# Four 64x64 tiles for strided attention and eight 64x32 tiles for two spans of local scores, with two PSUM banks in turn

## The chip, the cores and the metric

The kernel runs on one core of a Trainium2 chip. The metric is the device time of one execution in microseconds. Five engines work side by side: TensorE (PE in the rows; its weight loads are PEld), VectorE (DVE), ScalarE (ACT), GpSimd (POOL) and SyncE (SP), which here only issues DMAs. Each engine runs its own instructions in order; semaphores between them carry the dependencies.

## The reference: sparse attention, then a mixture of experts

Four batches of eight heads, 576 positions, head dimension 64. Heads 0 to 3 attend locally, to the last 32 positions; heads 4 to 7 attend with a stride, to earlier positions of the same remainder by 32. The 2304 rows that come out feed four experts.

```python
scores = scale * np.matmul(q, k.transpose(0, 1, 3, 2))
mask_local = (rel >= 0) & (rel < stride)
mask_strided = (rel >= 0) & (pos[None, :] % stride == pos[:, None] % stride)
scores = scores - np.max(scores, axis=-1, keepdims=True)
attn = np.exp(scores)
attn = attn / (np.sum(attn, axis=-1, keepdims=True) + 1e-09)
x = np.matmul(attn, v)                       # rearranged to (2304, 512)
h = np.maximum(x @ w1[e], 0.0)               # for each of 4 experts
out += p[:, e:e + 1] * (h @ w2[e])
```

## The kernel before

**Work.** Attention goes by 16 pairs of heads (4 batches x 4 pairs), in turn a local and a strided one. The two heads of a pair lie on partitions 0 to 63 and 64 to 127 of the tiles `qkL` and `qkS`, so a matmul of one head uses one half of TensorE's 128 rows. The experts are cut into 8 units of 512 hidden columns. The first 384 rows of x go through all 8 units while the attention of the other rows still runs (`plan_first`); the other 1920 rows follow in two parts after attention, with no attention in them.

**One pair.** `plan_pair` lays down, for each pair and for two parts of it (`gi`): the scores on TensorE into a PSUM bank of the pool `sc` (2 banks); on DVE the mask (which also empties the bank into `pm`) and the row maximum; the subtraction on DVE or POOL; the exponential on ACT; the row sum and its reciprocal on DVE; the normalization on DVE or POOL; a transpose (`tp`) on TensorE through the pool `ps` (2 banks), copied out by ACT or DVE; the values matmul (`pv`) into `ps`; and the copies out to `xh`, `xl` or `xr`.

**Tiles of the array.** In local scores a matmul has 64 rows and 32 columns; the two heads and two neighbouring blocks give four positions, (64h, 64h + 32i). In strided scores a matmul has 64x64 and head h stands at position (h, h): two positions. In strided values 54 of the 64 rows carry data; one part `gi` is one half `hf` of the rows, so its matmuls stand at (hf, 0) and (hf, 1): two positions. The part `gi` of strided scores (x in the changed code) and of strided values has one bank of its own.

**What sets the order.** Nothing is scheduled at run time. `Plan.walk` simulates the engines once while the kernel is built, with a cost for each operation, priorities in microseconds, banks in flight and a rule for taking turns between attention and experts on TensorE (`MIX`, `swing`, `ROW`), and writes out the instructions in the order of the simulated starts. The costs of the flexible operations also choose between DVE and POOL ("VP") and between ACT and DVE ("AD"). Early on it fills TensorE's waits with matmuls on zeros (`idle`, tile `wz`), up to `STEADY`.

**Names in rows.** A float32 matmul of attention is one row of the program but two instructions in the trace: 12 matmuls of the program are x24 in the trace. L494 is the local scores, L499 the strided scores, L556 the transposes, L583 the local values, L591 the strided values, L752 and L768 the experts' first and second matmuls over the first 384 rows, L921 those of the later parts, L1232 the zeros. Any matmul on the experts is called an expert matmul below.

Of the kernel before, what the change touches and what calls it, by code (L numbers as in the profile page):

```python
# [8 lines left out]
F32 = mybir.dt.float32  # L9
# [8 lines left out]
MIX = 0.8  # L18
# [5 lines left out]
LEAD = 11.15  # L24
LAG = 2.35
STEADY = 45.0
# [6 lines left out]
class Plan:  # L33
# [8 lines left out]
    DEEP = 1.3  # L42
    ROW = 1.51
# [3 lines left out]
    def __init__(self, banks, mix):  # L47
        self.ops = []
        self.writer = {}
        self.readers = {}  # L50
        self.banks = banks
        self.mix = mix
        self.swing = 2.0

    def add(self, eng, dur, fn, reads=(), writes=(), prio=0.0, bank=None, moe=False, cols=0, xfer=None, two=False, lead=None, lag=0.0):
# [7 lines left out]
        o.eng, o.dur, o.fn, o.prio, o.bank, o.moe = eng, dur, fn, prio, bank, moe  # L63
# [6 lines left out]
        o.idx = len(self.ops)  # L70
        pre = set()
# [33 lines left out]
    def walk(self):  # L105
# [31 lines left out]
        def fill(f, s, o):  # L137

            n = 0
            while True:  # L140
# [13 lines left out]
                if f + step > s and not forced:  # L154
# [9 lines left out]
        def when(o):  # L164
# [3 lines left out]
            if o.bank:  # L168
                n = len(allocs[o.bank[0]]) - self.banks[o.bank[0]]
                if n >= 0:  # L170
                    for p in self.readers.get(allocs[o.bank[0]][n], ()):
# [59 lines left out]
        while left:  # L231
# [20 lines left out]
            if e == "PE":  # L252
# [11 lines left out]
                if s < STEADY:  # L264
                    f = max(f, 1.07)
                    tag = next((t for t in allocs if not (o.bank and o.bank[0] == t) and clear(t, f) and not (began and t == "mo")), None)
# [6 lines left out]
            dur = took(o, e, s)  # L273
            if o.eng in self.FLEX:
# [26 lines left out]
            if o.bank:  # L301
                allocs[o.bank[0]].append(o.bank)
# [7 lines left out]
def attn_moe_kernel(  # L310
# [51 lines left out]
    const.tile([P, 8], F32, name="skew")  # L362
# [78 lines left out]
    def plan_pair(n):  # L441
# [11 lines left out]
        for gi in range(2):  # L453
            kb = (410, 213)[gi] if kd == "L" else 337
            add("SP", 0.65, lambda gi=gi: load_qk(n, gi), (), [f"qk{kd}{bf}{gi}"], zg[gi] - 16, xfer=((kb * 0.003, 128),), lead=lead)
# [5 lines left out]
        def pmv(g0, g1):  # L461
            if kd == "S":
                return pmx[:, g0:g1, 0:W]
            a = pmx[:, P * g0 + 1:P * g0 + 2]
            return bass.AP(a.tensor, a.offset, [list(a.ap[0]), [3 * P, (g1 - g0) // 3], [P + 32, 3], [1, W]])
# [12 lines left out]
        for gi, (g0, g1) in enumerate(GRP[kd]):  # L478
# [5 lines left out]
            def scores(key=key, gi=gi, g0=g0, g1=g1):  # L484
                s = bank(key)
                for g in range(g0, g1):
                    o = (g - g0) * W
                    for h in range(2):
                        a = slice(64 * h, 64 * h + 64)
                        if kd == "L":  # L490
                            o0, nq, _ = QKL[gi]
# [827 lines left out]
```

## Time and profile before

| | us |
|---|---|
| Median of 3 runs (804.46 to 805.23) | 804.83 |
| Profiled execution, its own time | 805.53 |
| Its span, first to last instruction | 803.7 |
| TensorE busy | 794.7 (99%) |
| VectorE busy | 612.9 (76%) |
| GpSimd busy | 357.3 (44%) |
| ScalarE busy | 330.4 (41%) |
| Share of TensorE in the chain that ended last | 96% |

TensorE is granted its full clock throughout (1.00 in every stretch asked for). A busy TensorE is not TensorE at its peak: small matmuls on few tiles of the array fill its time as well as large ones. So a gain is read from the time that passes between the first matmul of a piece and the first matmul of the next.

### The profile page before, as it was taken

What the parts mean: (1) busy time and instruction counts of PE and PEld (TensorE: products, weight loads), DVE (VectorE), ACT (ScalarE), POOL (GpSimd) and SP (SyncE); (2) the same over time, 40 slices, a digit from 0 to 9 for tenths busy, and PEclk for the clock granted to TensorE, in tenths of its full rate; (3) what the DMA queues carried; (4) which work ended last, traced back from release to release, by engine and by line L of the source; (5) the groups of instructions that cost most, each with busy time, mean ns of one, the idle gap of its engine ahead of it and who ended that gap; (6) DMA issues with size and microseconds to landing.
All of it is one profiled execution on the core that took longest, in us unless ns stands there. A gap on an engine that the chain in (4) does not pass through costs nothing.

```text
span 803.7 us, 13270 instructions
## 1 busy us (share of the span) xinstructions
PE 794.7 (99%) x5035; PEld 678.3 (84%) x5035; DVE 612.9 (76%) x871; ACT 330.4 (41%) x617; POOL 357.3 (44%) x277
## 2 busy tenths in 40 slices
PE   8999999999999999999999999999999999999998
PEld 5888888999889898888989888888888887888886
DVE  6888886875689776868687683868687878696986
ACT  3744646443336253444526361524131414232330
POOL 5442322932276451515244361526271808071762
PEclk9999999999999999999999999999999999999999
DMA  9675433348668696967764314838384747464625
GB/s 332 221 267 213 175 113 106 105 152 293 250 261 267 261 318 222 333 200 291 262 254 131 135 51 164 298 112 302 106 287 145 257 150 256 154 217 182 184 79 184
DMA packets 70400, 166.60 MB, mean 207 GB/s; under 512 B 5152, under 2 KB 23744, under 8 KB 70336
## 3 DMA queue, kind: packets, MB, share of 16 engines
q1 hardware_dynamic: 70192, 165.63, 58.8%
q8 instruction: 40, 0.66, 0.3%
q14 instruction: 24, 0.20, 0.1%
q10 hardware_dynamic: 144, 0.11, 0.0%
HBM read 105.94 MB, written 59.79 MB: 206 GB/s over the span
## 4 chain that ended last, share of the span: by engine, by line
PE 96%; DVE 2%; DMA 1%; ACT 1%; issue 0%; POOL 0%; DVEq 0%; ACTq 0%
PE mo L921 21%; PE mo L768 18%; PE ps L921 17%; PE sc L921 15%; PE mo L752 8%; PE sc L768 5%; PE ps L768 5%; PE ps L556 2%; PE ps L591 1%; PE sc L499 1%; DMA ring<-d23s 1%; PE sc L494 1%; PE ps L583 1%; PE mo L1232 1%; DVE wv L663 0%
## 5 line engine op out<-in xcount | busy, mean ns | idle before, releaser
L986 POOL TENSOR_TENSOR q<-q,q 128x512 f32<-128x512 f32 x41 | 60.9, 1494 | 143.2 <-DVE q L955 142.4
L768 PE MATMUL mo<-w2t,h 128*128 128x512 f32 x336 | 80.8, 389 | 0.0
L768 PEld LDWEIGHTS mo<-w2t,h 128*128 128x128 f32 x336 | 63.1, 188 | 13.0
L768 PE MATMUL mo<-w2t,hs 128*128 128x512 f32 x288 | 70.5, 396 | 0.0
L759 DVE SCALAR_TENSOR_TENSOR h<-c,h 128x448 fp32r<-128x448 f32 x48 | 61.3, 1305 | 2.4 <-ACT h L756 0.8
L768 PEld LDWEIGHTS mo<-w2t,hs 128*128 128x128 f32 x288 | 52.8, 188 | 11.0
L662 ACT ACTIVATE w2t<-raw 128x512 fp32r<-128x512 f32 x60 | 37.1, 630 | 41.9 <-PE mo L768 21.8
L663 POOL TENSOR_TENSOR a<-raw,a 128x512 fp32r<-128x512 f32 x19 | 29.8, 1570 | 52.8 <-DVE c L1124 48.0
L1035 DVE TENSOR_TENSOR acc<-sc,acc 128x512 f32<-128x512 f32 x58 | 39.2, 686 | 17.3 <-PE sc L921 17.2
L952 DVE TENSOR_TENSOR q<-ps,v 128x512 f32<-128x512 f32 x48 | 33.1, 690 | 24.9 <-PE ps L921 24.7
L777 DVE SCALAR_TENSOR_TENSOR acc<-mo,pr,acc 128x512 f32<-128x512 f32 x45 | 33.5, 745 | 22.3 <-PE mo L768 22.1
L943 ACT ACTIVATE v<-mo 128x512 f32<-128x512 f32 x48 | 28.6, 595 | 48.2 <-PE mo L921 48.2
L663 POOL TENSOR_TENSOR w2t<-raw,w2t 128x512 fp32r<-128x512 f32 x19 | 26.7, 1412 | 44.8 <-ACT w2t L662 44.8
L752 PE MATMUL mo<-xh,a 128*128 128x384 f32 x192 | 45.6, 341 | 0.0
L955 DVE SCALAR_TENSOR_TENSOR q<-q,pb 128x512 f32<-128x512 f32 x48 | 42.8, 892 | 1.6
L662 ACT ACTIVATE wv<-tmp 128x512 fp32r<-128x512 f32 x32 | 20.1, 632 | 54.6 <-POOL tmp L670 10.5
L768 PE MATMUL ps<-w2t,h 128*128 128x512 f32 x168 | 40.4, 389 | 0.0
L768 PE MATMUL sc<-w2t,h 128*128 128x512 f32 x168 | 40.4, 389 | 0.0
L981 ACT ACTIVATE Tb11h<-q 128x512 fp32r<-128x512 f32 x16 | 10.0, 628 | 71.5 <-DVE q L955 71.5
L663 DVE TENSOR_TENSOR w2t<-raw,w2t 128x512 fp32r<-128x512 f32 x41 | 35.1, 883 | 5.1 <-ACT w2t L662 5.1
L986 DVE TENSOR_TENSOR q<-q,q 128x512 f32<-128x512 f32 x23 | 32.7, 1421 | 6.7 <-POOL Tb21l L982 6.5
L768 PEld LDWEIGHTS sc<-w2t,h 128*128 128x128 f32 x168 | 31.5, 188 | 6.5
(270 smaller groups left out, 2109.0 us busy)
## 6 DMA issues: line engine op xcount, KB each, us to landing
raw<-in_w SPq DMA_DIRECT2D x30, 1024.0 KB, 6.1
qkS<-in_qk_strided SPq DMA_DIRECT2D x16, 329.0 KB, 6.5
out<-acc SPq DMA_DIRECT2D x18, 256.0 KB, 2.0
qkL<-in_qk_local SPq DMA_DIRECT2D x8, 400.0 KB, 6.5
vstL<-in_v_local SPq DMA_DIRECT2D x8, 384.0 KB, 7.0
vstS<-in_v_strided SPq DMA_DIRECT2D x8, 384.0 KB, 7.3
pb<-dp SPq DMA_DIRECT2D x5, 512.0 KB, 7.2
d17s<-s SPq DMA_DIRECT2D x4, 512.0 KB, 4.0
```

The costliest lines, as they stand in the source:

```text
L662: add("ACT", 0.62, lambda: nc.scalar.activation(out=hi(), in_=src(), func=AF.Copy), need, [name + "h"], z)
L663: add("VP", VP, lambda e: engine(e).tensor_tensor(out=lo(), in0=src(), in1=hi().bitcast(F32), op=ALU.subtract), need + [name + "h"], [name ...
L752: nc.tensor.matmul(pt[:, 0:TA], w[:, c % 2, (f % 2) * P:(f % 2) * P + P], (xl if i == 1 else xh)[c], start=j == 0, stop=j == 11)
L759: nc.vector.scalar_tensor_tensor(out=dst(), in0=src(), scalar=0.0, in1=hi().bitcast(F32), op0=ALU.max, op1=ALU.subtract)
L768: nc.tensor.matmul(pt, ht[f][:, ts], wt[f][:, cs], start=j == 0, stop=j == 11)
L777: nc.vector.scalar_tensor_tensor(out=a, in0=pt, scalar=sc, in1=a, op0=ALU.mult, op1=ALU.add)
L921: nc.tensor.matmul(pt, a[i == 2][:, j, f * P:f * P + P], skewed(b[i == 1][j], TH), start=bool(first) and n == 0, stop=True, skip_group_che ...
L943: add("ACT", TH2 / 1200 + 0.18, lambda: nc.scalar.activation(out=late["u"][i], in_=held[key][:, 0:TH2], func=AF.Copy), [key, "late3"], [f" ...
L952: add("DVE", DD, lambda: nc.vector.tensor_tensor(out=q(), in0=src(), in1=late["u"][i], op=ALU.add), [key, f"u{i}", "late3"], [tok], min(zz ...
L955: add("DVE", DD, lambda: nc.vector.scalar_tensor_tensor(out=q(), in0=q() if from_q else src(), scalar=0.0, in1=late["p"][:, c * TH2:c * TH ...
L986: add("VP", VP, lambda e: engine(e).tensor_tensor(out=dst[0](), in0=a[0](), in1=b[0](), op=ALU.subtract), [a[1], b[1]], [dst[1]], zz - 2.4)
L1035: add("DVE", DD, lambda i=i, key=key: nc.vector.tensor_tensor(out=acc[i], in0=held[key][:, 0:TH2], in1=acc[i], op=ALU.add), [key], tok, zd)
```

## The change

**Strided scores.** The two parts of a pair become one operation. It takes two `sc` banks at once, one for each head (that is, for each half of the rows). Each step issues four matmuls at four positions: part x at columns 64x, head h at rows 64h. The host lays out `qkS` accordingly: halves of the pair that were on x now come before the heads.

**Strided values.** The two parts become one operation too, with two `ps` banks, one for each half `hf` of the rows; each step issues matmuls at (hf, h), four positions.

**Local scores.** The first part of a pair covers two spans of three blocks (v = 0, 1); it takes two `sc` banks, one for each span, and the second span swaps the heads' column halves (`h ^ v`), so that eight 64x32 positions are used. The second part has one span and keeps four positions. The mask of the first part is now two instructions of 189 elements where one of 378 stood; transposes and values read the swapped halves.

**Sums.** The local row sum reads one more column, which holds 1e-9 from the start (two small memsets on POOL), and the separate addition of 1e-9 (16 instructions on DVE) is gone.

**The start.** The exponential's table is loaded by a dummy exponential after the masks' DMA is issued. The first block of w1 comes in two DMAs of half the size. In SP's order the first local pair's v and the first half of w1 now stand behind all four strided loads of q and k, before behind two of them. The second quarter of it that is split is now s3's, ahead of a12's.

**The plan.** `MIX`, `swing`, `ROW`, `STEADY`, `LEAD`, `LAG`, `DEEP` and the costs of attention's operations have other values; a switch from attention to experts costs 0.17 in the plan; at most ten zero matmuls are put in at a time beyond the start; and `SHIFT` moves the due times of 70-odd operations. The built program has 21 zero matmuls where it had 18. From the middle of the experts' first rows on (the last 3,050 of some 4,290 expanded rows) TensorE's program is the same.

```diff
-MIX = 0.8
+MIX = 0.85
+ZN = 30
+ZR0, ZR1 = 26.0, 24.0
-LEAD = 11.15
-LAG = 2.35
-STEADY = 45.0
+LEAD = 8.24
+LAG = 1.8
+STEADY = 30.04
+SHIFT = {
+    3: 5.5, 31: 1.9, 32: 1.8, 42: 1.7, 52: 10.9, 58: -4.8, 59: -4.8, 67: -4.8, 78: -7.5, 79: -14.4, 87: -6.6, 88: -3,
...
-    DEEP = 1.3
-    ROW = 1.51
+    DEEP = 1.27
+    ROW = 1.98
+    SWITCH = 0.17
+    FIRST = 10
+    SWING = 4.72
...
+            keys = [key]
+            if kd == "S":
+                keys = [("sc", n, "b", i) for i in range(2)] if gi == 0 else []
+            elif gi == 0:
+                keys = [("sc", n, "b", 0), ("sc", n, "b", 2)]
+
+            def scores(keys=keys, gi=gi, g0=g0, g1=g1):
+                ss = [bank(x) for x in keys]
+                if kd == "S":
+                    for o in range(0, 6 * W, W):
+                        for x in range(2):
+                            for h in range(2):
+                                a = slice(64 * h, 64 * h + 64)
+                                nc.tensor.matmul(
+                                    ss[h][64 * x:64 * x + 64, o:o + W], qkv[a, x, o:o + 64],
+                                    qkv[a, x, QKS + o:QKS + o + SR], start=True, stop=True)
+                    return
+                o0, nq, _ = QKL[gi]
+                for r in range(3):
+                    for v, s in enumerate(ss):
+                        for h in range(2):
                             for i in range(2):
-                                t = o0 + 96 * (2 * ((g - g0) // 3) + i) + 32 * (g % 3)
+                                a = slice(64 * h, 64 * h + 64)
+                                t = o0 + 96 * (2 * v + i) + 32 * r
+                                p = 64 * (h ^ v) + 32 * i
                                 nc.tensor.matmul(
-                                    s[64 * h + 32 * i:64 * h + 32 * i + 32, o:o + W], qkv[a, t:t + 32],
+                                    s[p:p + 32, r * W:r * W + W], qkv[a, t:t + 32],
                                     qkv[a, t + nq + 1:t + nq + 1 + W], start=True, stop=True)
-                        else:
-                            lhsT, rhs = qkv[a, gi, o:o + 64], qkv[a, gi, QKS + o:QKS + o + SR]
-                            nc.tensor.matmul(s[a, o:o + W], lhsT, rhs, start=True, stop=True)
...
-                    nc.vector.tensor_reduce(out=rows(sm, g0, g1), in_=pmv(g0, g1), op=ALU.add, axis=AX.X)
-                    nc.vector.tensor_scalar_add(out=r, in0=r, scalar1=1e-9)
+                    nc.vector.tensor_reduce(out=rows(sm, g0, g1), in_=pmv(g0, g1, 1), op=ALU.add, axis=AX.X)
...
+                if kd == "S":
+                    for j in range(6):
+                        for h in range(2):
+                            for hf in range(2):
+                                r, c0 = slice(64 * hf, 64 * hf + SR), 64 * (j % 2)
+                                nc.tensor.matmul(
+                                    oo[hf][64 * h:64 * h + 64, j * SR:j * SR + SR], vv[r, h, j, :],
+                                    pt[r, 3 * h + j // 2, c0:c0 + SR], start=True, stop=True)
+                    return
...
+        for j in range(2):
+            add("SP", 0.4, lambda j=j: load_w(which, u, slice(2 * j, 2 * j + 2)), (), [toks[j]], Z0 - (ZR0, ZR1)[j], xfer=((1.45, 256),), lag=LAG)
...
-        for src, nm in ((A11, "a11"), (A12, "a12"), (A21, "s3"), (A22, "a22")):
-            plan_quarter(src, "raw1", nm, z)
+        for src, nm, j in ((A11, "a11", 0), (A21, "s3", 0), (A12, "a12", 1), (A22, "a22", 1)):
+            plan_quarter(src, f"raw1{j}", nm, z)
...
         nc.scalar.dma_start(out=both, in_=c_masks)
+        nc.scalar.activation(out=warm[:, 0:1], in_=wz[:, 0:1], func=AF.Exp)
```

In the middle of attention, on TensorE before (`vstS` is the strided values' v, `qkL` and `qkS` local and strided q and k, `hs` the experts' hidden rows):

```order
209 L591 MATMUL ps<-pTS,vstS_241 64x54 x24
210 L768 MATMUL mo<-w2t,hs_223 128x512 x2
211 L768 MATMUL mo<-w2t,hs_227 128x512
212 L768 MATMUL mo<-w2t,hs_224 128x512 x2
213 L768 MATMUL mo<-w2t,hs_228 128x512
214 L556 MATMUL ps<-ident,pmL_242 128x128 x6
215 L494 MATMUL sc<-qkL_235 32x63 x12
216 L499 MATMUL sc<-qkS_237 64x54 x12
```

At about the same place now:

```order
218 L622 MATMUL ps<-pTS,vstS_241 64x54 x24
219 L529 MATMUL sc<-qkL_235 32x63 x12
220 L529 MATMUL sc<-qkL_234 32x63 x12
221 L630 MATMUL ps<-pTL,vstL_238 64x96 x8
222 L817 MATMUL mo<-w2t,hs_225 128x512 x2
223 L817 MATMUL mo<-w2t,hs_229 128x512
224 L817 MATMUL mo<-w2t,hs_226 128x512 x2
225 L817 MATMUL mo<-w2t,hs_230 128x512
226 L592 MATMUL ps<-ident,pmS_244 128x128 x3
227 L592 MATMUL ps<-ident,pmL_243 128x128 x3
228 L517 MATMUL sc<-qkS_237 64x54 x24
```

A pair's strided scores stand in one piece of 24 where they came as 12 and 12 in two places, and four pieces of attention follow one another before the experts' next turn.

On POOL before, from the first strided softmax to the low parts of the first w1 block (`a_77` is the quarter a11, `s_80` s3, `a_78` a12, `a_79` a22):

```order
18 L516 TENSOR_TENSOR pmS_244<-pmS_244,mx 128x6x54
19 L516 TENSOR_TENSOR pmL_243<-pmL_243,mx 128x2x3x63
20 L532 TENSOR_TENSOR pmS_244<-pmS_244,sm 128x6x54
21 L663 TENSOR_TENSOR a_77<-raw_202,a_77 128x512
22 L663 TENSOR_TENSOR a_78<-raw_202,a_78 128x512
23 L663 TENSOR_TENSOR s_80<-raw_202,s_80 128x512
24 L663 TENSOR_TENSOR a_79<-raw_202,a_79 128x512
```

The same place on POOL now:

```order
21 L562 TENSOR_TENSOR pmL_243<-pmL_243,sm 128x2x3x63
22 L547 TENSOR_TENSOR pmS_244<-pmS_244,mx 128x6x54
23 L562 TENSOR_TENSOR pmL_242<-pmL_242,sm 128x3x63
24 L562 TENSOR_TENSOR pmS_244<-pmS_244,sm 128x6x54
25 L547 TENSOR_TENSOR pmL_243<-pmL_243,mx 128x3x63
26 L707 TENSOR_TENSOR s_80<-raw_202,s_80 128x512
27 L707 TENSOR_TENSOR a_77<-raw_202,a_77 128x512
```

More softmax stands ahead of the first w1 quarter, s3's low part goes before a11's, and a22's has moved to DVE.

On ACT at the start, before:

```order
1 L1162 DMA both<-c_masks 128x432
2 L520 ACT_TABLE_LOAD
3 L520 ACTIVATE pmL_242<-pmL_242 128x2x3x63
4 L520 ACTIVATE pmL_242<-pmL_242 128x3x63
5 L433 ACTIVATE pTL<-ps 128x384 x2
```

and now:

```order
1 L1211 DMA both<-c_masks 128x432
2 L1212 ACT_TABLE_LOAD
3 L1212 ACTIVATE warm<-wz 128x1
4 L551 ACTIVATE pmL_242<-pmL_242 128x2x3x63
5 L551 ACTIVATE pmL_243<-pmL_243 128x2x3x63
6 L452 ACTIVATE pTL<-ps 128x384 x2
```

The table load stands in front of the dummy, whose operand is ready early, and no longer in front of the first exponential.

## Rows read from the trace of the kernel before

**Rows 1.** Stretches: length, busy us of PE, PEld, DVE, ACT, POOL (instructions), granted clock.

```profile
20.00:60.00 40.00, 39.23 (x591) 34.67 (x586) 35.46 (x84) 23.52 (x51) 20.02 (x22) 1.00 0.69 243
60.00:120.00 60.00, 60.00 (x945) 50.93 (x944) 51.58 (x116) 32.08 (x73) 17.92 (x24) 1.00 0.47 169
...
200.00:804.00 604.00, 598.90 (x2718) 509.51 (x2716) 459.08 (x571) 227.06 (x402) 271.90 (x185) 1.00 0.60 210
```

**Rows 2.** TensorE in order of time, 49 to 64: start, us, line, count.

```profile
49.85 0.53 PE L494 MATMUL sc<-qkL 64*32 64x63 f32 x24
50.32 0.91 PE L499 MATMUL sc<-qkS 64*64 64x54 f32 x24
51.16 0.96 PE L752 MATMUL mo<-xh,a 128*128 128x384 f32 x4
...
53.44 1.21 PE L583 MATMUL ps<-pTL,vstL 128*64 128x96 f32 x24
54.58 0.91 PE L499 MATMUL sc<-qkS 64*64 64x54 f32 x24
...
58.38 0.86 PE L494 MATMUL sc<-qkL 64*32 64x63 f32 x48
59.17 0.55 PE L556 MATMUL ps<-ident,pmL 128*128 128x128 f32 x3
...
61.77 1.43 PE L591 MATMUL ps<-pTS,vstS 54*64 54x54 f32 x48
63.12 1.19 PE L768 MATMUL mo<-w2t,hs 128*128 128x512 f32 x4
```

**Rows 3.** The same view, 117 to 128.

```profile
117.33 0.91 PE L591 MATMUL ps<-pTS,vstS 54*64 54x54 f32 x24
118.17 0.96 PE L752 MATMUL mo<-xh,a 128*128 128x384 f32 x4
...
127.30 0.55 PE L583 MATMUL ps<-pTL,vstL 128*64 128x96 f32 x8
127.78 0.55 PE L556 MATMUL ps<-ident,pmS 128*128 128x128 f32 x3
```

**Rows 4.** Stretches of L591 alone: length, busy us (matmuls under way), clock, DMA, GB/s.

```profile
19.30:19.82 0.52, 0.52 (x18) 1.00 1.01 380
19.82:20.00 0.18, 0.18 (x20) 1.00 1.04 389
```

**Rows 5.** L591 in 19 to 21: count, duration ns min/median/max, first and last start.

```profile
L591 PE MATMUL ps<-pTS,vstS x48: 218/218/258, 19.3 to 20.5; 54*64 54x54 f32 x48
```

**Rows 6.** DVE groups in the first 134 us: line, tiles, count, busy us, mean ns.

```profile
L510 DVE TENSOR_TENSOR pmS<-sc,both 128x324 f32<-128x324 f32 x16 | 7.7, 482 | 0.1
...
L510 DVE TENSOR_TENSOR pmL<-sc,both 128x378 f32<-128x378 f32 x8 | 4.3, 543 | 6.8 <-PE sc L494 6.8
...
L526 DVE TENSOR_SCALAR sm<-sm 128x3 f32<-128x3 f32 x8 | 3.2, 394 | 0.3
...
L510 DVE TENSOR_TENSOR pmL<-sc,both 128x189 f32<-128x189 f32 x8 | 2.8, 349 | 0.4 <-PE sc L494 0.3
L526 DVE TENSOR_SCALAR sm<-sm 128x6 f32<-128x6 f32 x8 | 1.9, 240 | 0.3
```

**Rows 7.** All engines in order of time, 8 to 20.

```profile
8.61 1.28 ACT L520 ACT_TABLE_LOAD   x1 [8.61 <-DVE pmL L516]
...
16.73 2.84 POOL L663 TENSOR_TENSOR a<-raw,a 128x512 fp32r<-128x512 f32 x2
...
18.07 0.42 PE L752 MATMUL mo<-xh,a 128*128 128x384 f32 x1
```

**Rows 8.** Waits of TensorE: line, releaser, us in total, times, longest.

```profile
PE ps L556 <- DVE xl L630: 0.3, 1, 0.3
PE ps L1183 <- DVE xl L630: 0.3, 1, 0.3
PE ps L556 <- POOL pmS L532: 0.2, 1, 0.2
```

More of the change, by code (lines that the diff above doesn't have):

```diff
@@ L70, in add @@
         o.idx = len(self.ops)
+        o.prio += SHIFT.get(o.idx, 0.0)
         pre = set()
@@ L153, in fill @@
                     need - o.cols) / 2400 / rate > rem - max(s - f, 0.0) - o.dur / rate
-                if f + step > s and not forced:
+                if f + step > s and not forced or not out and n >= self.FIRST:
                     return n, f
@@ L167, in when @@
                 t = max(t, wire - self.DEEP)
-            if o.bank:
-                n = len(allocs[o.bank[0]]) - self.banks[o.bank[0]]
+            for i, key in enumerate(o.bank):
+                n = len(allocs[key[0]]) - self.banks[key[0]] + i
                 if n >= 0:
-                    for p in self.readers.get(allocs[o.bank[0]][n], ()):
+                    for p in self.readers.get(allocs[key[0]][n], ()):
                         if p.start is None:
@@ L265, in walk @@
                     f = max(f, 1.07)
-                    tag = next((t for t in allocs if not (o.bank and o.bank[0] == t) and clear(t, f) and not (began and t == "mo")), None)
+                    tag = next((t for t in allocs if not (o.bank and o.bank[0][0] == t) and clear(t, f) and not (began and t == "mo")), None)
                     n, f2 = fill(f, s, o) if tag else (0, f)
@@ L273, in walk @@
             dur = took(o, e, s)
+            if e == "PE" and o.moe and last[e] is not None and not last[e].moe:
+                dur += self.SWITCH
             if o.eng in self.FLEX:
@@ L300, in walk @@
                     offer(x)
-            if o.bank:
-                allocs[o.bank[0]].append(o.bank)
+            for key in o.bank:
+                allocs[key[0]].append(key)
             out.append((s, o.idx, 0, fn))
@@ L537, in plan_pair @@
             vp = (dd, nel * 1.6e-3 + 0.22)
-            add("PE", 0.2 + ng * (0.107, 0.116)[c > 1], scores, [f"qk{kd}{bf}{gi}"], [key, tok], z + 3, key, cols=(4, 2)[c > 1] * nel)
-            add("DVE", dd, mask, [key, "mask" + kd], [tok], z + 3.2)
+            if kd == "S" and gi == 0:
+                add("PE", 0.9, scores, [f"qkS{bf}{i}" for i in range(2)], keys + [f"pmS{bf}{i}" for i in range(2)], z + 3, keys,
+                    cols=4 * nel)
+            elif kd == "L":
+                add("PE", (0.5, 0.46)[gi], scores, [f"qkL{bf}{gi}"], keys + [tok], z + 3, keys, cols=4 * nel)
+            for i, x in enumerate(keys if kd == "L" else [key]):
+                a0, a1 = (g0 + 3 * i, g0 + 3 * i + 3) if kd == "L" else (g0, g1)
+                add("DVE", (a1 - a0) * W / 960 + 0.15, lambda x=x, a0=a0, a1=a1: mask(x, a0, a1), [x, "mask" + kd], [tok], z + 3.2)
             add("DVE", dd, rmax, [tok], [tm], z + 3.4)
@@ L647, in attn_moe_kernel, with load_w @@
     NU = len(units)
-    def load_w(which, u):
+    def load_w(which, u, ks=slice(0, NKD)):
         e, f = units[u]
         src = w1[e, :, f * FH:(f + 1) * FH] if which == 1 else w2[e, f * FH:(f + 1) * FH, :]
-        nc.sync.dma_start(out=raws[which], in_=src.rearrange("(k p) f -> p k f", p=P))
+        nc.sync.dma_start(out=raws[which][:, ks], in_=src.rearrange("(k p) f -> p k f", p=P)[:, ks])
     def raw_quarter(i, j, which=1):
```

109 lines of the change are left out of this document (53 added, 56 removed), and 5 rows, old and new, of the table SHIFT.

## The prediction, made before the changed kernel was run

> **What bounds the kernel now.** I read the busy time by stretch first. TensorE works 60.00 of 60.00 us while attention and experts share it and 598.90 of the last 604 us without attention; the clock is 1.00 in both [rows 1]. So from about 20 us on the end moves by what TensorE's own pieces cost, and DVE (35.46 of 40 us, then 51.58 of 60) is the engine that would be late next. I then read TensorE in order of time, and took as the price of a piece the distance from its first matmul to the first of the next piece: a duration as printed includes a matmul's way through the array, which the next piece overlaps. Last I read the start, where TensorE waits and its pieces cost nothing.
>
> **Prices of the pieces before.** Strided scores of half a pair, x24: 50.32 to 51.16, 0.84 us, and the same at 54.58 [rows 2]. Local scores: 0.47 us for the part with one span (x24, 49.85 to 50.32), 0.79 us for the part with two (x48, 58.38 to 59.17) [rows 2]. Local values x24: 1.14 us (53.44 to 54.58) [rows 2]. Strided values of a pair at once, x48: 1.35 us (61.77 to 63.12) [rows 2]; half of one, x24: 0.84 us (117.33 to 118.17) [rows 3].
>
> **Do four tiles run at once?** The trace of before already has it for a moment. When the two parts of strided values follow each other, the second stands on the other half of the rows, with a bank of its own, and starts before the first has ended. From its beginning the first runs alone, and 18 matmuls start in 0.52 us, 35 a us; in the 0.18 us where both run, 20 are under way [rows 4]. A matmul of this line takes 0.22 us from start to end [rows 5], so about 8 of the 20 (35 x 0.22) had started before the stretch, and 12 start in it: 67 a us, about twice as many. That is the doubling, for 64x64 tiles, on both row halves, into the same PSUM partitions of two banks. That is the very form that the strided values and scores get.
>
> In the half piece of strided values all matmuls stand in one half of the rows, on two column tiles, and it costs 0.84 us [rows 3], the same as strided scores on two different halves of the rows [rows 2]; so two column tiles of one row half do not hinder each other. [...]
>
> **The change, part by part.**
> Strided scores. A pair issues 48 instructions over four tiles, as many rounds as 24 over two: 0.84 us for two pieces of 0.84. Over 8 pairs this is 8 x 0.84 = 6.7 us less. Bounds: 0 (no more than two tiles at once) and 6.7.
> Strided values. Seven pairs go from 1.35 to 0.84 (7 x 0.51 = 3.6), one that was in two halves from 1.68 to 0.84 (0.8): 4.4 us less; bounds 0 and 4.4.
> Local scores with two spans. 48 instructions over eight tiles are as many rounds as 24 over four: 0.79 to 0.47, 8 x 0.32 = 2.6 us less. No row shows eight tiles, nor four column tiles in one row half busy with both halves; so bounds 0 and 2.6, and I take 2.6, because the four-tile form already has both halves write one bank with no loss against its own part with one span (0.32 us more for twice the work).
> Local values. The same work, but the new order cuts it 8 and 4 in five pairs, before in two. A cut costs what a piece has beside its stream: x24 takes 1.14 [rows 2] and x8 takes 0.48 (127.30 to 127.78) [rows 3], so 0.33 per x8 and 0.15 per cut: 3 x 0.15 = 0.45 us more.
> Attention done ahead of the experts. What TensorE does before its first expert matmul costs nothing, as it waits there anyway. In the new order this holds one more half pair of strided scores, six more transposes and eight more local values matmuls, and by the prices above it grows by about 0.5 us: 0.5 us less behind it; bounds 0 and 1.
> The first expert matmul, at 18.07 before [rows 7]. Two pieces leave the softmax chain ahead of it: the exponential's table load, 1.28 us, which stood between the subtraction and the first exponential [rows 7], and the separate 1e-9, 0.24 to 0.39 us [rows 6]. But the third expert matmul needs the low part of the first w1 quarter, and POOL made that from 16.73 on, at 1.4 us each [rows 7]. In POOL's new order more softmax and s3's low part stand ahead of it; on SP the v of the first local pair and the w1 block now go behind four strided loads of q and k where only two stood ahead, though w1 comes in two halves. Bounds: 1.7 us earlier (both pieces gained) and 1.4 later (one more split). I take 0.3 earlier: the chain's gain less a split.
> DVE. The 16 additions go (3.2 + 1.9 = 5.1 us), 16 masks of 349 ns stand for 8 of 543: 1.2 us more [rows 6]. The new order also has nine fewer subtractions and normalizations on DVE, about 0.5 us each, and as many more on POOL, busy 17.92 of 60 [rows 1]. On a bound TensorE this is worth nothing by itself; it is the cover for the next term.
> Waits between 18 and 134 us. Before, 0.3 + 0.3 + 0.2 = 0.8 us [rows 8]. Now TensorE asks for the same softmax results in a stretch some 13 us shorter, and a two-bank operation must wait until both banks are emptied; behind it in TensorE's queue stand the experts' matmuls. DVE works 87.0 of the 100 us from 20 to 120 [rows 1]; without the 3.9 and some 4.5 that went to POOL it has 78.6 to do in about 87: 90%, little above the 87% it had. I take 1.5 us of waits, 0.7 more than before; bounds 0 and 5, that is 0.8 less and 4.2 more.
> Zero matmuls, 21 for 18: they fill waits, so nothing, unless a wait they stand in ends early (0.2 us each).
> Behind attention TensorE's order is the same and I take nothing.
>
> Sum: -6.7 - 4.4 - 2.6 + 0.45 - 0.5 - 0.3 + 0.7 = -13.35, say **-13.4 us**. The profiled execution took 805.53 us with a span of 803.7; the sum gives it 792.1, with a span of 790.3. The median, 804.83, lies 0.7 under the profiled run; the same difference gives **791.4 us**. Own range: the first expert matmul and the waits at their good bounds (1.4 and 1.5 better) give 788 with the rounding; waits of 4 us give 794.
>
> **Rivals.**
> (a) Eight tiles take turns. Four column tiles in one row half might not load and stream at once; then local scores stay at 0.79 and the time is 791.4 + 2.6 = 794.0. For it: no row has it; against it: four tiles of 64x32 lose nothing. Chance 0.08.
> (b) The tiles of one row half take turns (or the new positions do not run side by side for another reason). Then scores, values and local scores gain nothing: 791.4 + 13.7 = 805.1. For it: the stretch with four tiles is 0.18 us long [rows 4]; against it: that stretch, and the half piece at 0.84 [rows 3]. [...] Chance 0.04.
> (c) DVE and POOL become the bound of the shared stretch. If TensorE waits for softmax 6.5 us instead of 1.5, as 90% on DVE with a fixed order allows, the time is 791.4 + 5 = 796. For it: DVE's 35.46 of 40 at the start [rows 1], where every wait of TensorE is on DVE or POOL [rows 8]; against it: waits were 0.8 us in all. Chance 0.13.
> (d) Slower: two banks at once take away the turn between banks. The pool for scores has two banks, and after a two-bank operation TensorE cannot begin the next scores until DVE has masked both. Two masks of 482 ns [rows 6] are 1.0 us; 8 strided and 8 local scores and 8 strided values are 24 such places, and if all were exposed 24 us would come on top: 791.4 + 24 = 815. It decides from 13.4 / 24 = 0.56 us per place on. Against it: in the order expert matmuls or transposes stand between most such pieces. Chance 0.03.
>
> **How the numbers follow.** My forecast has 0.72. Its own range with its tails left out and (a) hold somewhat under 0.80, so the range goes on into (c): **788 to 797**. A measurement of this kernel tells about 0.2% (1.6 us) from no change. Faster by more: forecast, (a) and (c), 0.93. Within: (b), 0.04. Slower: (d), 0.03.
>
> **What would show it.** In the changed profile: strided scores and values of a pair as x48 at 0.84 us to the next piece, local scores with two spans at 0.47; the first expert matmul at 17.8; waits of TensorE of 1.5 us after it; the last strided values ending some 15 us earlier than before (six expert matmuls fewer stand ahead of them); the stretch behind 200 us as full as now. Strided pieces at 1.3 us or more would make the mechanism wrong; pieces at 0.84 with TensorE waiting for masks or normalizations would leave the mechanism right and the sum wrong.

## The result and the profile after

The changed kernel takes 795.28 us (median of 4 runs, 794.87 to 796.09), the kernel before in the same session 805.03 us (4 runs, 804.46 to 806.61): a ratio of 0.9877, 95% interval 0.9860 to 0.9894. It is faster by 9.8 us (1.2%). The forecast was 791.4 with a range of 788 to 797: direction, mechanism and range held, but the time lies 3.9 us above the forecast. Of these, 3.1 are span (793.4 where 790.3 was forecast). The other 0.8 come from carrying a profiled execution over to a median: before, the median lay 0.7 below the profiled execution; now it lies 0.1 above it.

Span and busy time of each engine:

```profile
span 793.4 us, 13252 instructions
...
PE 784.8 (99%) x5038; PEld 667.8 (84%) x5038; DVE 602.7 (76%) x854; ACT 330.6 (42%) x617; POOL 366.1 (46%) x289
```

The busy time by stretch, to be laid beside [rows 1] (length, busy us of PE, PEld, DVE, ACT, POOL with instructions, granted clock, DMA share, GB/s):

```profile
20.00:60.00 40.00, 39.27 (x615) 33.75 (x615) 35.40 (x80) 23.72 (x52) 21.31 (x25) 1.00 0.72 258
60.00:120.00 60.00, 59.07 (x994) 50.74 (x991) 46.61 (x106) 35.83 (x78) 21.16 (x28) 1.00 0.49 173
```

TensorE is still the bound. It idles for 0.93 us between 60 and 120, where it had no gap before, and DVE, the engine feared in rival (c), has become lighter (46.61 us instead of 51.58).

TensorE in order of time, as in [rows 2] (start, us, line, count). L517 is the strided scores now, L529 the local scores, L592 the transposes, L622 the strided values, L630 the local values, L801 and L817 the first and second expert matmuls:

```profile
56.18 0.92 PE L517 MATMUL sc<-qkS 64*64 64x54 f32 x48
57.03 0.55 PE L592 MATMUL ps<-ident,pmL 128*128 128x128 f32 x3
...
60.74 0.72 PE L529 MATMUL sc<-qkL 64*32 64x63 f32 x48
61.39 0.55 PE L592 MATMUL ps<-ident,pmL 128*128 128x128 f32 x3
```

Strided scores of a whole pair go from 56.18 to 57.03: 0.85 us for x48, where x24 took 0.84. (A price is again the distance to the next piece; the second number of a row is the duration.) Local scores with two spans go from 60.74 to 61.39: 0.65 us. Before it was 0.79, forecast was 0.47. The five of the eight such pieces that other work follows at once take 0.651 to 0.653 us.

**Where the 10.3 us of span went.** I summed the same distances over three stretches. The first expert matmul begins at 19.26 instead of 18.07: 1.2 us lost. From there to the first expert matmul behind the last strided values (121.65, before 133.42) it takes 102.4 us instead of 115.3: 13.0 us gained, namely strided scores 6.6, strided values 4.1, six expert matmuls that moved behind this stretch 1.4 and the rest 0.9. Behind it: 671.7 us instead of 670.3, which are the same six expert matmuls. Without rounding, 12.96 - 1.19 - 1.42 = 10.35. The two parts of 6.6 and 4.1 are rough: in two places of the kernel before, the last matmuls of the values and the first of the scores alternate, and a wait of 0.3 us stands behind each place [rows 8]. With the prices of undisturbed pieces, values give 4.4, scores 5.8 (half a pair of them moved ahead), and some 0.5 are those waits. The first expert matmul now (before, [rows 7]):

```profile
19.26 0.44 PE L801 MATMUL mo<-xh,a 128*128 128x384 f32 x1
```

The waits of TensorE between 18 and 134 us, as in [rows 8], and one stretch in order of time:

```profile
PE ps L630 <- issue: 0.9, 1, 0.9
PE ps L592 <- DVE xl L674: 0.7, 1, 0.7
```

```profile
69.45 0.92 PE L622 MATMUL ps<-pTS,vstS 54*64 54x54 f32 x48
70.30 0.86 PE L529 MATMUL sc<-qkL 64*32 64x63 f32 x48
71.23 0.46 PE L630 MATMUL ps<-pTL,vstL 128*64 128x96 f32 x5
72.56 0.71 PE L630 MATMUL ps<-pTL,vstL 128*64 128x96 f32 x11 [0.86 <-issue]
```

The longest wait stands in the middle of a piece and nothing that the profile knows releases it ("issue"). Strided values, local scores (here two one-span parts, x24 each) and local values follow each other without an expert matmul between. TensorE goes through the first two, 192 instructions, in 1.8 us, and stops after five matmuls of the third (the trace has one instruction for each matmul and one for its weight load, 5038 of each in the list of engines above).

So three things had to be settled by experiment: whether the turn over four tiles is the gain; why the local scores gained so little; and where 1.2 us at the start and 0.86 us at 71.7 come from.

### The profile page after: what moved, and what is told of

Same layout as the page of the kernel before. It is cut to its first block, busy times and chain, and to the rows that moved or that the text cites. A ratio compares the mean times of both kernels' runs of the same rounds, so it can differ in the third digit from the quotient of the medians.

```text
span 793.4 us, 13252 instructions
## 1 busy us (share of the span) xinstructions
PE 784.8 (99%) x5038; PEld 667.8 (84%) x5038; DVE 602.7 (76%) x854; ACT 330.6 (42%) x617; POOL 366.1 (46%) x289
## 4 chain that ended last, share of the span: by engine, by line
PE 97%; DMA 1%; DVE 1%; issue 0%; ACT 0%
PE mo L970 22%; PE mo L817 18%; PE ps L970 17%; PE sc L970 15%; PE mo L801 9%; PE ps L817 5%; PE sc L817 5%; PE ps L592 2%; PE ps L630 1%; DMA ring<-d23s 1%; PE sc L529 1%; PE ps L622 1%; PE sc L517 1%; PE mo L1282 1%; DVE wv L707 0%
## 5 line engine op out<-in xcount | busy, mean ns | idle before, releaser
L817 PE MATMUL mo<-w2t,h 128*128 128x512 f32 x336 | 80.8, 389 | 0.0
L817 PEld LDWEIGHTS mo<-w2t,h 128*128 128x128 f32 x336 | 63.1, 188 | 13.0
L817 PE MATMUL mo<-w2t,hs 128*128 128x512 f32 x288 | 70.0, 396 | 0.0
L817 PEld LDWEIGHTS mo<-w2t,hs 128*128 128x128 f32 x288 | 52.9, 188 | 11.2 <-DVE hs L808 0.3
L707 POOL TENSOR_TENSOR a<-raw,a 128x512 fp32r<-128x512 f32 x17 | 27.0, 1590 | 53.3 <-DVE c L1173 38.4
L707 POOL TENSOR_TENSOR w2t<-raw,w2t 128x512 fp32r<-128x512 f32 x20 | 28.6, 1436 | 44.9 <-ACT w2t L706 43.9
L801 PE MATMUL mo<-xh,a 128*128 128x384 f32 x192 | 45.7, 341 | 0.0
L817 PE MATMUL ps<-w2t,h 128*128 128x512 f32 x168 | 40.4, 389 | 0.0
L817 PE MATMUL sc<-w2t,h 128*128 128x512 f32 x168 | 40.4, 389 | 0.0
L817 PEld LDWEIGHTS ps<-w2t,h 128*128 128x128 f32 x168 | 31.5, 188 | 6.5
```

The source lines that it names most:

```text
L707: add("VP", VP, lambda e: engine(e).tensor_tensor(out=lo(), in0=src(), in1=hi().bitcast(F32), op=ALU.subtract), need + [name + "h"], [name ...
L801: nc.tensor.matmul(pt[:, 0:TA], w[:, c % 2, (f % 2) * P:(f % 2) * P + P], (xl if i == 1 else xh)[c], start=j == 0, stop=j == 11)
L817: nc.tensor.matmul(pt, ht[f][:, ts], wt[f][:, cs], start=j == 0, stop=j == 11)
```

## The experiments

**1. Two tiles at a time in the new order.** Both loops of the strided operations are turned so that only two tiles take turns in one step. In the values they are the two that took turns before; in the scores they are two row halves over one column half, where before they stood at (0, 0) and (1, 1):

```diff
-                    for o in range(0, 6 * W, W):
-                        for x in range(2):
+                    for x in range(2):
+                        for o in range(0, 6 * W, W):
                             for h in range(2):
...
-                    for j in range(6):
-                        for h in range(2):
-                            for hf in range(2):
+                    for hf in range(2):
+                        for j in range(6):
+                            for h in range(2):
```

> The changed kernel with the loops of strided scores and strided values turned round, so that only two tiles take turns at a time, as before; banks, order of the pieces and everything else as changed. Theory (the turn over four tiles carries the gain): strided scores x48 go from 0.85 to about 1.54 us, strided values from 0.85 to about 1.36; 8 x 0.69 + 8 x 0.51 = 9.6 us more, about 805, the time of the kernel before. Rival (the new order of the pieces carries it, the pieces would overlap in any case): pieces stay near 0.85 and the time within 1.5 us of 795.3.

Measured: 801.96 us median (800.82 to 802.61; ratio to before 0.9955, 0.9939 to 0.9971). TensorE in order of time:

```profile
58.39 1.43 PE L517 MATMUL sc<-qkS 64*64 64x54 f32 x48
59.75 0.55 PE L592 MATMUL ps<-ident,pmL 128*128 128x128 f32 x3
...
73.11 1.43 PE L622 MATMUL ps<-pTS,vstS 54*64 54x54 f32 x48
74.46 0.86 PE L529 MATMUL sc<-qkL 64*32 64x63 f32 x48
75.26 1.25 PE L630 MATMUL ps<-pTL,vstL 128*64 128x96 f32 x16
76.44 0.73 PE L817 MATMUL mo<-w2t,hs 128*128 128x512 f32 x2
```

A piece of strided scores takes 1.36 us, strided values the same: 8 x 0.51 for each of the two, 8.1 us in all. The turn over four tiles is worth that; the rival (order) falls. The span is only 6.6 us longer than with the change, because the two waits of 0.9 and 0.7 us in the change's list are not there. But the time does not go back to 804.9. I had expected 1.54 for scores; in one piece they cost 1.36 where two halves cost 1.68, as strided values before cost 1.35 in one piece [rows 2] and 0.84 a half [rows 3]. There the second half begins while matmuls of the first are under way [rows 4]; that it does so here too is my estimate from these prices. So of the 0.83 us that a pair of strided scores gained, 0.51 is the turn over four tiles, and 0.32 is the joining of two pieces (on other tile positions than before, which no run tells apart from it).

**2. Four tiles at a time in local scores.**

```diff
-                for r in range(3):
-                    for v, s in enumerate(ss):
+                for v, s in enumerate(ss):
+                    for r in range(3):
```

> The changed kernel with only the two spans of local scores one after the other, so that four tiles take turns instead of eight. Theory: the piece x48 goes from 0.652 back to 0.79 us, 8 x 0.14 = 1.1 us more, 796.4. Rival (eight tiles give nothing, 0.652 comes from the two banks or from what stands beside it): the piece stays at 0.65 and the time at 795.3.

Measured: 795.75 us (795.04 to 797.47; ratio 0.9886, 0.9866 to 0.9906), no difference from the change that can be measured. TensorE in order of time:

```profile
60.34 0.77 PE L529 MATMUL sc<-qkL 64*32 64x63 f32 x48
61.04 0.55 PE L592 MATMUL ps<-ident,pmL 128*128 128x128 f32 x3
```

The piece takes 0.695 us, between both theories. Of the 0.14 us that it gained, 0.10 comes with the second span on other tiles and in a bank of its own (the two are not told apart); that the spans overlap where they meet is my estimate, no row shows it. Eight tiles in turn add only 0.043.

**3. Local scores twice over.**

```diff
-                for r in range(3):
+                for r in (0, 1, 2) * (1 + (len(ss) == 2)):
```

> The changed kernel with every matmul of the two-span local scores issued twice over (the three row thirds, then the same three again), so a piece has 96 matmuls in the trace. It tells why the piece takes 0.652 us and not 0.47. Theory (supply: 32 matmuls lie ready, the rest comes at 16.7 ns each): the slow part begins after 32 matmuls again and lasts to the end, 64 x 16.7 ns, piece 1.4 to 1.5 us, time about 802. Rival (the last third of the rows is slow by its place in the banks): a slow part in the middle and one at the end, piece about 1.15 us, time about 799.5. Rival (no limit, only a late start of the last third): 0.98 us, about 798.

Measured: one run, 803.63 us. TensorE in order of time, and then the part of it from 40.55 to 40.80 alone:

```profile
40.56 1.17 PE L529 MATMUL sc<-qkL 64*32 64x63 f32 x96
41.65 0.55 PE L592 MATMUL ps<-ident,pmL 128*128 128x128 f32 x3
```

```profile
40.56 0.45 PE L529 MATMUL sc<-qkL 64*32 64x63 f32 x32
```

The piece takes 1.10 us: none of the three prices. The first 32 matmuls start within 0.24 us, eight per 55 ns; on four tiles, in the kernel before, four start per 55 ns (L494 from 49.85); so eight tiles do run at once. Then, by the single starts, comes a halt of some 0.08 us, and from there eight start per 67 ns, 8.3 ns for one matmul with its weight load, in the second pass through the same tiles and banks as in the first. Three short groups are slower, at 16 to 18 ns a start: right behind the halt, in the middle and at the end; what slows them stays open. So it is not the place of the last third, and not 16.7 ns throughout, which I had read from the thin tail of a piece: in the dense part one matmul and one weight load come per 8.3 ns after the first 32. In a piece of x48 the last 16 fall into that halt and the slower stream, half of them at 15 to 18 ns: 0.65 instead of 0.47 us. Experiment 9 shows the same 8.3 ns with matmuls of another kind.

The profile of this kernel holds a second result. Its span is 8.1 us longer than with the change, of which the doubled pieces behind the first expert matmul explain some 2.7 and the start 5.1:

```profile
9.27 0.47 PE L517 MATMUL sc<-qkS 64*64 64x54 f32 x15
13.10 1.12 PE L517 MATMUL sc<-qkS 64*64 64x54 f32 x33 [3.36 <-issue]
```

```profile
14.00:20.00 6.00, 6.00 (x105) 4.24 (x103) 4.33 (x14) 2.24 (x6) 3.15 (x5) 0.60 1.01 348
```

TensorE stops for 3.4 us in the middle of strided scores that had nothing to wait for, and the granted clock is 0.60 from 14 to 20 us (columns as in [rows 1]). The profile of the changed kernel lists what fits this, a DMA queue of its own for instructions (queue, kind: packets, MB, share of 16 engines):

```profile
q8 instruction: 40, 0.66, 0.3%
```

In the changed kernel, 40 packets of 16 KB for some 10,200 rows of TensorE in the trace are 255 rows each. I then counted TensorE's rows up to each pause of over 0.2 us that is put down to "issue", up to 134 us, in the changed kernel and the nine of the experiments: at all 19 the count is 193 over a multiple of 256 or up to four rows less (449 and 2497 in the changed kernel; 449, 1729, 2497 and 3009 in this one, that is 1280, 768 and 512 apart, or 5, 3 and 2 times 256). So I take 256 rows for a block. And each of these pauses ends 1.25 to 1.61 us after a packet of that queue has landed: here 10.59 to 11.69, then 13.10; in the changed kernel 70.05 to 71.14, then 72.56. At every border of a block up to 134 us, paused or not, in all eleven traces (168 of them), the first instruction comes 1.25 us or more after its packet has landed; at all but five of the 149 without a pause it is 1.78 us or more. The kernel before has none of these pauses; its closest border has 1.79 us. So I read the wait without a name as TensorE waiting for its next block of instructions; of the 168 borders 19 show it as a pause.

**4. The planner's constants of before.** `MIX`, `LEAD`, `LAG`, `STEADY`, `DEEP`, `ROW` and the swing as before, no shifts of single steps (`SHIFT` has 60, not 70-odd as said above) and no `SWITCH` and `FIRST`; the tiles, banks and the costs of the operations as changed:

```diff
-MIX = 0.85
+MIX = 0.8
...
-LEAD = 8.24
-LAG = 1.8
-STEADY = 30.04
+LEAD = 11.15
+LAG = 2.35
+STEADY = 45.0
...
+SHIFT = {}
```

> The changed kernel with the planner's constants of before (its shares of attention and experts, its load lead, its limits, no shifts of single steps), so the pieces stay as cheap as changed and only their order goes back to the rule of before. Theory of the prediction (on a full TensorE the order is worth little): 795 to 798, TensorE waits 1 to 4 us after the first expert matmul. Rival (the new constants carry a good part of the gain): above 799, with TensorE waiting for softmax or transfers, or the first expert matmul later than 19.26.

Measured: 800.69 us (800.20 to 802.35; ratio 0.9944, 0.9927 to 0.9962). The rival holds. From 14 to 45 us TensorE is busy for 26.64 of 31 us, with eleven zero matmuls among it, where the change has 30.02 with four. Its waits there:

```profile
PE ps L1226 <- DVE pr L1214: 1.3, 1, 1.3
PE mo L794 <- DVE xl L667: 1.3, 2, 1.1
PE ps L585 <- DVE xl L667: 1.2, 2, 0.9
PE ps L585 <- POOL pmS L555: 0.3, 1, 0.3
```

```profile
14.91 0.44 PE L794 MATMUL mo<-xh,a 128*128 128x384 f32 x1
```

The first expert matmul stands at 14.91, 4.4 us earlier than with the change, and the kernel is 5.4 us slower. Part of the early start is no gain: one pair's strided scores (x48), twelve transposes and local values x16, which the change does ahead of it, come behind it here. Another part is waits, as TensorE asks earlier for what DVE and POOL deliver: 4.3 us and eleven zero matmuls, where the change has 1.6 us and one zero matmul from its first expert matmul on. So about half of the change's gain exists only with the new constants, whose order has few such waits; which of the constants does it was not tested.

**5. 46 instructions more.** The last zero matmul, at 25.3 us in a wait, becomes 24 small ones:

```diff
+        if len(fills) == 7:
+            for i in range(24):
+                a, b = 0, 32 * (i % 4)
+                nc.tensor.matmul(t[b:b + 32, 8 * i:8 * i + 8], wz[a:a + 32, 0:32], wz[a:a + 32, 0:8], start=True, stop=True)
+            return
```

> The changed kernel with the last zero matmul, near 25.3 us where TensorE waits anyway, in place of which stand 24 small ones (32x32 weights, 8 columns): 46 instructions more on TensorE at no cost of its own or nearly so. Theory (the pause of 0.86 us at 71.7 us is TensorE waiting for its next block of 256 instructions): the border of the block moves 46 instructions up the program, out of the dense row of strided values and local scores, and the pause is gone or under 0.3 us; every pause that remains falls where the instructions executed so far are 193 over a multiple of 256; span 792.5, time about 794.4. Rival (the pause belongs to the local values: their operands, banks or the eviction beside them): it stays between the same instructions with 0.8 to 0.9 us, time 795.3.

Measured: 794.57 us (794.23 to 794.81; ratio 0.9865, 0.9850 to 0.9879). TensorE in order of time:

```profile
69.50 0.92 PE L622 MATMUL ps<-pTS,vstS 54*64 54x54 f32 x48
70.35 0.64 PE L529 MATMUL sc<-qkL 64*32 64x63 f32 x31
72.06 0.46 PE L529 MATMUL sc<-qkL 64*32 64x63 f32 x17 [1.07 <-issue]
72.45 0.88 PE L630 MATMUL ps<-pTL,vstL 128*64 128x96 f32 x16
```

The pause moved out of the local values into the middle of the local scores, 46 instructions up, as theory had it; the rival (something in the local values) falls. It did not get shorter (1.07 us): the border still lies in the same dense row. The time is not told apart from the change.

**6. The first quarter of w1 ahead of the third.** One shift is left out:

```diff
-    326: -24.5, 336: -24.5, 432: 4.2, 433: 2.6, 445: 10.9, 447: 6.8, 899: 4.2, 900: 2.6, 922: 10.9, 924: 6.8,
+    326: -24.5, 336: -24.5, 432: 4.2, 445: 10.9, 447: 6.8, 899: 4.2, 900: 2.6, 922: 10.9, 924: 6.8,
```

> The changed kernel without the planner's shift of one step, the rounding of the first w1 quarter on ScalarE, so that ScalarE and GpSimd take that quarter before the third (a11 ahead of s3). Theory (the first expert matmul stands at 19.26 because this quarter is made last): it begins at 18.0 to 18.3 and the two zero matmuls at 17.6 go; what follows is in another order, so the end gains at most that 1.0 us: 794.3 to 796. Rival (the start is set by softmax and transposes): the first expert matmul stays at 19.0 or later.

Measured: 798.45 us (797.10 to 799.40; ratio 0.9909, 0.9888 to 0.9930). POOL makes the quarter `a` first (from 16.21), and the expert matmuls begin 1.7 us earlier than with the change. TensorE in order of time, and the longest of its waits up to 134 us:

```profile
17.53 0.42 PE L801 MATMUL mo<-xh,a 128*128 128x384 f32 x1
```

```profile
PE ps L630 <- issue: 2.0, 2, 1.6
PE ps L630 <- DVE xl L674: 1.3, 1, 1.3
PE sc L529 <- DVE pmL L541: 0.8, 2, 0.4
PE ps L592 <- ACT xr L682: 0.8, 1, 0.8
```

So the late first expert matmul of the change is the order of two splits, as suspected. But the time, expected at 794.3 to 796, is 3.2 us worse than the change. Part of it is waits: the 1.3 and 0.8 us on DVE and ACT between 22 and 26 us and 0.7 more at the pause for instructions (1.6 instead of 0.9). Another part is the clock (columns as in [rows 1]):

```profile
22.00:26.00 4.00, 1.89 (x86) 1.51 (x79) 3.83 (x13) 3.75 (x10) 1.96 (x3) 0.99 0.86 266
26.00:29.30 3.30, 3.30 (x14) 3.20 (x13) 3.25 (x5) 2.10 (x5) 2.73 (x3) 0.50 0.50 192
```

TensorE is busy for 1.89 of 4.00 us, and then the granted clock is 0.50 for 3.3 us; by my estimate from these two numbers this costs half of them, some 1.7 us. In the change it is 1.00 in both stretches. Of the four executions the one with a mean clock of 1.00 was the fastest (797.10), still slower than the change.

**7. Without the early exponential.**

```diff
-        nc.scalar.activation(out=warm[:, 0:1], in_=wz[:, 0:1], func=AF.Exp)
```

> The changed kernel without the early small exponential, so that the table load stands again between the first subtraction and the first exponential. It prices the term of the prediction that this load leaves the softmax chain. Theory (the chain up to the first expert matmul is softmax): first exponential about 1.2 us later than 8.48, first expert matmul 0.5 to 1.3 us later than 19.26, time 795.8 to 796.6. Rival (the chain is GpSimd's weights, instruction supply or transfers, and the load hides): first expert matmul within 0.2 us of 19.26.

Measured: one run, 796.13 us, 0.85 more than the median of the change and 0.04 above the slowest of its four runs, so the time alone shows little. The first exponential moves from 8.48 to 9.93 behind the table load (1.28 us), the first expert matmul from 19.26 to 20.35. The load lies on the chain to the first expert matmul: 1.1 us there, of which the span shows 0.7 (794.1 against 793.4).

**8. 154 instructions more at the start.** Each of the first 11 zero matmuls is cut in eight:

```diff
-            nc.tensor.matmul(t, wz[:, 0:P], wz, start=True, stop=True)
+            for o in range(0, 512, w):
+                nc.tensor.matmul(t[:, o:o + w], wz[:, 0:P], wz[:, o:o + w], start=True, stop=True)
```

> The changed kernel with each of the first 11 zero matmuls cut into eight of 64 columns: the same columns, 154 instructions more on TensorE before the first scores. Theory (pauses are the wait for a block of 256 instructions): the pause at 71.7 us is gone, since its border moves 154 instructions up; the first border comes after 295 instead of 449 of the old instructions, at about 9.5 us, and as the start's fetch has begun between 10.3 and 11.7 us in all kernels so far, TensorE pauses there until about 13 us; first expert matmul 2 to 4 us later, time 796.5 to 799. Rival (the pause at 71.7 belongs to the work there): it stays at the same instruction with 0.8 to 0.9 us, and the start has no new pause; time 795.3 to 796.

Measured: one run, 795.53 us. TensorE in order of time around the place of the pause, and its waits from 2 to 22 us:

```profile
71.75 0.92 PE L622 MATMUL ps<-pTS,vstS 54*64 54x54 f32 x48
72.61 0.86 PE L529 MATMUL sc<-qkL 64*32 64x63 f32 x48
73.55 0.88 PE L630 MATMUL ps<-pTL,vstL 128*64 128x96 f32 x16
```

```profile
PE sc L517 <- issue: 2.3, 2, 1.2
PE ps L630 <- ACT pTL L452: 0.5, 2, 0.3
```

The same dense row runs through without a pause, and two pauses of 1.1 and 1.2 us stand at the start instead, at row counts of 447 and 702. The first expert matmul comes at 21.80, 2.5 us later, and the stretch to the last strided values is 1.4 us shorter. The time was expected at 796.5 to 799 and is below that: the later start costs less than it is long, since the stretch behind it gains the pause back and more. The work at 71 us is innocent; where the border of a block falls decides.

**9. The same 154 instructions behind the start.** 78 small zero matmuls in the slot of experiment 5, in place of 24.

> The changed kernel with 78 small zero matmuls (32x32 weights, 4 columns) in place of the last zero matmul near 25.3 us: 154 instructions more, as many as in the kernel with the first zero matmuls cut in eight, but behind the start. Theory: the start is that of the changed kernel (pause near 13.1, first expert matmul at 19.2 to 19.3), and from 30 to 125 us the borders of the 256-instruction blocks fall where they fell in that other kernel, where no pause was left; so no pause over 0.2 us there. The small ones take 78 x 6.4 ns = 0.5 us of a slot of 0.4: span 793.4 - 0.9 + 0.1 = 792.6, time about 794.4. Rival (a pause comes wherever strided values and local scores stand together, at any border): a pause of 0.5 us or more between 60 and 80 us, span 793.2 or more.

Measured: 796.99 us (796.80 to 799.06; ratio 0.9895, 0.9879 to 0.9912), where 794.4 was expected; the profile is of the slowest of the four executions. TensorE in order of time, and the stretch behind it (columns as in [rows 1]):

```profile
29.71 0.90 PE L622 MATMUL ps<-pTS,vstS 54*64 54x54 f32 x42
...
32.77 0.33 PE L622 MATMUL ps<-pTS,vstS 54*64 54x54 f32 x6 [2.15 <-issue]
```

```profile
32.00:40.00 8.00, 7.23 (x80) 6.68 (x80) 4.06 (x9) 3.69 (x9) 1.99 (x2) 0.79 0.54 186
```

From 60 to 80 us there is no pause, as expected. But the small matmuls are themselves a dense row: they use up 156 instructions in 0.67 us, and the next border, at count 1217, is reached before its block is there. TensorE stops for 2.15 us, and behind the pause the granted clock is 0.79 over 8 us; the first pause of the start was also 1.1 instead of 0.33 us. By their single starts the first 37 small matmuls come four per 25 ns, 6.3 ns apart, all others four per 33 ns, 8.3 ns: the rate of the dense part in experiment 3, with 4 columns each instead of 63.

No version beat the change by more than a measurement can tell; experiment 5 has the lowest median, within 0.1%.

## Why the prediction held, and where it missed

- **Four tiles at once.** Right: 0.85 us for x48 where 0.84 was forecast, for scores and values. Behind the first expert matmul they give 10.6 us together; by undisturbed prices values give the 4.4 that was forecast and scores 5.8, of which 0.84 is the half pair that now stands ahead of it. What the prediction did not see is that 0.32 us of each pair of scores comes from joining the two pieces; its rival (b) at 805.1 set the case without concurrency too slow, since experiment 1 measures 801.96 (with the 1.1 us that local scores keep there, some 803.1 by my estimate).
- **Local scores, -2.6.** This is the step of the sum that failed: "48 instructions over eight tiles are as many rounds as 24 over four". Eight tiles do run at once, for 32 matmuls; then a matmul with its load comes per 8.3 ns at best, whether it has 63 columns or 4 (experiments 3 and 9). That this is the rate at which TensorE gets its instructions is my reading of it, which no run shows by itself. 0.14 us a piece instead of 0.32 gives 1.1 us; 1.5 us of the forecast are missing here. Rival (a), tiles that take turns, is not what happened.
- **First expert matmul, 17.8.** It came at 19.26: "the chain's gain less a split" had the right parts and mis-sized them. Against before, the chain gained 0.5 us with the quarter first (17.53 in experiment 6 against 18.07) where the prediction had up to 1.7; the table load alone is worth 1.1 (experiment 7), and part of it is eaten by a pause of 0.33 us for instructions at 13.14; the rest I did not separate. The split in the wrong place costs 1.7 where 1.4 was the bound. Together 1.2 later instead of 0.3 earlier: the other 1.5 us. That this term adds to the end one for one is itself doubtful: in experiments 4 and 6 an earlier start came with a slower kernel, and in 7 and 8 a start 1.1 and 2.5 us later came with a span only 0.7 and 0.4 us longer.
- **Waits, 1.5 us.** The size held (0.9 + 0.7) by luck, the kind did not. Only the 0.7 is a wait on DVE, the sort that the prediction spoke of; the 0.9 is a wait for instructions, a resource that appears nowhere in the prediction. Making pieces twice as dense is what brought it in: the piece of local values in which it stands takes 1.96 us with the change, 1.18 us in experiment 1, which has the same instructions in the same pieces at two tiles a step, and 0.81 us where no border falls into it.
- **Rivals (c) and (d).** Neither came. Behind the first expert matmul no wait on a mask stands in the list, so two banks at once hide. (c) shows its face in experiment 4: with the order of before, DVE is what TensorE waits for.
- **Order.** The prediction put the new order near zero (-0.5, +0.45, +0.7). As a forecast of what the given order does this was fair; as a statement on its worth it was wrong, since without the new constants the same tiles give 800.69. The cuts of the local values cost what was forecast (0.81 + 0.48 for 16 and 8 against 1.14 for 24).
- **Behind attention.** As forecast, no change but the six expert matmuls.
- **The range.** 795.28 lies outside the 788 to 794 that the prediction gave for its own mechanism. It is within 788 to 797 only because the range went on into rival (c), which did not come; the part above 794 was filled by two mis-sized terms, local scores and first expert matmul, that both missed to the same side. That the range held is partly luck.

What stays open: why a block of instructions comes as late as it does. At the 19 pauses its packet starts 2.7 to 4.4 us after the first instruction of the block before it; where the DMA engines are quiet it often starts within 1 us (61.72 against 60.91 in the changed kernel, DMA share 0.19 from 60 to 64; 70.05 against 66.91 at a share of 1.05 from 66 to 70). All 168 borders up to 134 us in the eleven traces fit this. The packet starts more than 2 us after that instruction at 73 of them, the 19 pauses included, and there the DMA engines were busy at a share of 0.51 or more in between (0.80 or more at the pauses); where the share was under 0.5 it started 1.53 us after it at the latest. That a packet stands behind bulk loads is my estimate from these shares; no run changed the loads alone.

## What to carry to other kernels

In these runs small matmuls on distinct tiles of the array ran side by side, column tiles of one row half included (0.85 us for x48 on four tiles), down to 8.3 ns for a matmul with its load: below that, price them by this rate and not by the array. When such pieces are made denser, look for "issue" pauses in the middle of a piece and count instructions to them. Where the pieces themselves were slower, at two tiles a step (experiment 1), the pause was 0.3 us instead of 0.9; that slow matmuls between dense pieces help too is my estimate from this, no run tried it by itself. And a cheaper piece on the bound engine was only half a gain here until the order was planned anew for it.

## What the runs showed that I had not expected

- TensorE waits for its own instructions: in blocks of 256, 0.2 to 3.4 us at a time, with 1.25 to 1.61 us between the landing of a block and its first instruction.
- A matmul of 4 columns and one of 63 columns on small tiles come at the same 8.3 ns behind the first 32 to 37, and these at 6.3 to 6.9 ns.
- A pause of 3.4 us (experiment 3) is followed by a granted clock of 0.60 from 14 to 20 us, and one of 2.15 us (experiment 9) by 0.79 over 8 us. In experiment 6 two waits of 1.3 and 0.8 us close together are followed by 0.50 over 3.3 us. The pauses of 0.3 to 1.2 us in the changed kernel and in experiment 8 left it at 1.00.
- A first expert matmul 4.4 us earlier came with a kernel 5.4 us slower.
